# Layout of the reloaded product spectra: group of four token tiles ahead of sequence half

## The chip, the cores and the metric

The kernel runs on 1 core of one Trainium2 chip. The metric is the device time of one execution in microseconds (us); lower is better.

## The reference

One layer works on a sequence of 2048 tokens of 512 channels, in bfloat16:

```python
x = A_u                                   # (1, 2048, 512)
xn = _layernorm(x, axis=-1)
return x + A(xn) + B(xn)

# A: a state space convolution along the sequence, for each channel
P = exp(dt * A_cplx * l)                  # (512, 128, 2048): 128 modes
K = einsum("dn,dnl,dn->dl", C, P, dt * B).real
Yf = rfft(xn.T, padded to 4096) * rfft(K, padded to 4096)
y = irfft(Yf)[:, :2048].T + xn * Dskip

# B: a gated feed-forward of width 1792
h = sigmoid(xn @ w_gate) * (xn @ w_up)
y = h @ w_down
```

## The kernel before, in words

Three streams of work are woven into one program. The feed-forward runs over 4 groups of 512 tokens: gate matmuls (line 1030), up matmuls (line 1054), their products, and down matmuls (line 1098). The filter's spectrum is generated on the chip. The convolution is done with transforms written as matmuls. The step that matters here is its last one, the inverse transform.

**Products.** For each half of the channels (`p`, 0 or 1, 256 channels each) and each of 8 steps `u`, the product spectrum is made on TensorE (line 935), copied out of PSUM by ScalarE or VectorE (helper lines 283 and 285), and stored to a scratch tensor `v_scr` in HBM (dma helper, line 417). The inverse transform needs the same numbers with another index on the partitions, so they are read back in another order. This is the "reload".

**Reload.** The buffer `vall` lies at the start of `big`, the one large SBUF tile out of which most temporary buffers are cut by byte offset. It has, for each partition, `p`, a sequence half `j` (2), a token tile `i` (16) and 256 channels: 32 KB per partition. The reload comes in 12 transfers. There are three parts (`VPART`): part 0 is channel half 0 on all 128 partitions (512 KB a transfer), part 1 is channel half 1 on partitions 0 to 95 (384 KB), part 2 is channel half 1 on partitions 96 to 127 (128 KB). Each part has four transfers, one for each group of four token tiles; below "group 0" is tiles 0 to 3, "group 3" is tiles 12 to 15. A transfer brings both sequence halves of its four tiles: for each partition two pieces of 2 KB, one for each `j`.

**Inverse transform.** `s2_mm` (line 989) makes one token tile: for each `j` one matmul of 64 output rows (line 994), which reads tile `i` of both channel halves at once, 2 x 256 numbers that lie 16 KB apart. Tiles 12 to 15 get one matmul more (line 996). `final` makes two tiles: four matmuls into a pair of PSUM banks, then an addition on VectorE (line 1009), then the store of the result. Tiles 12 to 15 are added to the down matmuls' banks instead (lines 1104 and 1108), and VectorE adds the input (line 1118).

**Order.** `ORDER` lists all operations by hand in the order in which they are issued; each engine and each DMA queue takes its own in that order and never overtakes. For the reload, the SyncE queue (SP) has in this order: part 0 groups 2, 3, 0; part 2 groups 0, 2; part 1 groups 0, 3, 2; then part 0 group 1 and part 1 group 1; product stores stand between the first of them, and stores of the result behind the last. Part 2 groups 3 and 1 are on ScalarE's queue. TensorE's last operations are, in this order: 28 down matmuls; tiles 2 and 3 (group 0, four matmuls); tile 12 (group 3); tiles 0 and 1 (group 0); tile 13; tiles 8 and 9 (group 2); 14 down matmuls; tiles 6, 7, 4, 5 (group 1); tiles 14, 15; tiles 10 and 11; 28 half-width down matmuls.

**Waits.** Nobody writes a wait in this kernel. The tile framework compares the stretches of memory that two operations touch, and where they overlap and one of them writes, it makes the later one in the program wait for the earlier one. A wait of a DMA stands at the head of its queue and holds all transfers behind it.

Of the kernel before, what the change touches and what calls it, by code (L numbers as in the profile page):

```python
# [13 lines left out]
ACT = mybir.ActivationFunctionType  # L14
# [9 lines left out]
NT = 16  # L24
# [12 lines left out]
NP, DW = 2, 256  # L37
# [260 lines left out]
def _rate(pkt):  # L298

    pkt = min(pkt, 2048)  # L300
    return 16e3 * pkt / (pkt / 26.5 + 8.5)
# [14 lines left out]
def kernel(  # L316
# [12 lines left out]
    V, S, T, P, Y = nc.vector, nc.scalar, nc.tensor, nc.gpsimd, nc.sync  # L329
# [47 lines left out]
    def at(off, shape, dt=BF):  # L377
        assert off % 32 == 0
        n = int(np.prod(shape)) * (4 if dt == F32 else 2)
        assert off + n <= NBIG, (off, n)  # L380
        v = big[:, off // 2:(off + n) // 2]
        if dt == F32:
            v = v.bitcast(F32)
        if len(shape) > 1:
            ax = ["a%d" % i for i in range(len(shape))]
            v = v.rearrange("p (%s) -> p %s" % (" ".join(ax), " ".join(ax)), **dict(zip(ax[1:], shape[1:])))
        return v

    o = 0
# [7 lines left out]
    s2 = at(OFF["tmp"], [2, 64])  # L397
# [11 lines left out]
    def dma(q, dst, src, deps=(), prio=0.0, acq=(), rel=(), pkt=1024, after=None, hv=0.5):  # L409

        n = None
        get = lambda v: v() if callable(v) else v
        holder = {}

        def fn():
            with nc.allow_non_contiguous_dma(reason="laid out"):
                holder["i"] = QUEUE[q].dma_start(out=get(dst), in_=get(src))
            if after:
                after(holder["i"])

        return lambda nbytes: pl.add(q, 0.62, fn, deps, prio, acq, rel, dma=(nbytes, _rate(pkt), hv))
# [324 lines left out]
    for c in range(4):  # L746
# [10 lines left out]
        n = 1  # L757
# [214 lines left out]
    o_rt = pl.add("PE", 0.32, f_rt, [o_rz], 60, acq=[slr])  # L972
    o_rz = pl.add("ACT", 0.48, lambda slr=slr: S.activation(out=rr[0:8, :], in_=bank(slr)[0:8, :], func=ACT.Identity), [o_rt, l_sr, m_rr], 60, rel=[slr])

    vall = at(0, [NP, 2, NT, DW])
    vl = []
    for t in range(0, 8, 2):
        lds = []
        for n, (p, u0, u1) in enumerate(VPART):
            v_v = v_scr[n][:].rearrange("g q d -> (g q) d").rearrange("(p j i) d -> p j i d", j=2, i=NT)  # L980
            lds.append(dma("ACT" if n == 2 and t % 4 else "SP", vall[16 * u0:16 * u1, p, :, 2 * t:2 * t + 4, :], v_v[:, :, 2 * t:2 * t + 4, :],
                           deps=v_st[n] + table_free, prio=20 + n + 0.01 * t, pkt=2048, hv=0.9)(64 * KB * (u1 - u0)))
        vl.append(lds)
    vp_op = [vl[t // 2] for t in range(8)]
# [4 lines left out]
    def s2_mm(t, r, o, start, w):  # L989
        kw = dict(stop=True, skip_group_check=True)  # L990
        i = 2 * t + r
        ps = slice(w[0] // DW, w[1] // DW)
        for j in range(2):
            T.matmul(o[64 * j:64 * j + 64, :], s2[:, r, :], vall[:, ps, j, 2 * t + r, :], start=start, tile_position=(0, 64 * j), **kw)  # L994
        if i >= 12:
            T.matmul(o[64:128, :], sr[:, i - 12, :], rr[:, w[0]:w[1]], start=False, tile_position=(0, 64), **kw)

    def final(t, gdeps):
        sl, osl = _Slot("s"), _Slot("ot")
        ot = lambda: at(TAIL["ot"] + osl.idx * 2 * KB, [2, D])  # L1000

        def fy():
            for r in range(2):
                s2_mm(t, r, bank(sl, r), True, (0, D))
        my = pl.add("PE", 0.45, fy, vp_op[t] + [l_s2], 30 + t * 0.01, acq=[sl], mode="H")

        def fe():
            res = glu_sb[:, 2 * t:2 * t + 2, :] if t < 4 else at(TAIL["glu"] + 2 * KB * (t - 4), [2, D])
            V.tensor_tensor(out=ot().rearrange("p r d -> p (r d)"), in0=two(sl), in1=res.rearrange("p r d -> p (r d)"), op=ALU.add)  # L1009
        fin = pl.add("DVE", 1.13, fe, [my] + gdeps, 30, acq=[osl], rel=[sl])  # L1010
        isl = slice(2 * t, 2 * t + 2)
        dma("SP", outv[:, isl, :], lambda: ot(), deps=[fin], prio=1, rel=[osl], pkt=2048)(256 * KB)

    for grp in range(4):
# [63 lines left out]
        for jj in range(4):  # L1078
# [10 lines left out]
            r = jj % 2  # L1089
# [3 lines left out]
            def f2(i, po, c, start):  # L1093
                s2_mm(i // 2, i % 2, bank(po)[:, 0:c[1] - c[0]], start, c)
# [92 lines left out]
```

## Time and profile before

| what | value |
|---|---|
| median of 3 runs (lowest to highest) | 246.4 us (246.3 to 247.63) |
| profiled execution's own time | 246.36 us |
| its span, first to last instruction | 244.4 us |
| mean granted TensorE clock | 0.955 |
| TensorE matmul busy | 222.4 us, 91% |
| VectorE / ScalarE busy | 205.6 us, 84% / 174.7 us, 71% |
| GpSimd busy | 18.6 us, 8% |
| reload transfers `big<-v_scr` in the chain that ended last | 7% of the span |

Times in the profile count from the start of the span. "SPq" and "ACTq" are the sequencers of SyncE and ScalarE, where DMAs are issued; "PE" is TensorE, "DVE" VectorE, "ACT" ScalarE, "POOL" GpSimd. In the chain of waits a row is start, length, and what the time went to; a DMA's length there runs from its issue until its data have landed. A row of the timeline is start, length, engine, line, operation, tiles, count, and in brackets the idle time ahead of it and what ended it.

### The profile page before, as it was taken

How to read it: one execution, taken by the hardware profiler on the slowest of the kernel's cores; microseconds unless marked ns; L12 is line 12 of the kernel's file. 1: busy time of each engine (PE TensorE's matmuls, PEld its weight loads, DVE VectorE, ACT ScalarE, POOL GpSimd, SP SyncE). 2: the span in 40 equal slices, each digit the busy share in tenths (PEclk: the TensorE clock that was granted, in tenths of full speed). 3: DMA queues.
4: the chain of work that ended last, by engine and by line, in shares of the span. 5: the costliest groups of instructions: out<-in, count | busy, mean ns of one | idle time of the engine just before them, and what ended most of it. 6: DMA issues, size and time to landing. Idle time of an engine off the chain costs nothing.

```text
span 244.4 us, 5428 instructions
## 1 busy us (share of the span) xinstructions
PE 222.4 (91%) x2120; PEld 112.4 (46%) x2120; DVE 205.6 (84%) x448; ACT 174.7 (71%) x282; POOL 18.6 (8%) x42
## 2 busy tenths in 40 slices
PE   7969999999999999999999999999999999801694
PEld 3544444444444464465555664565536554300243
DVE  3999889999999999999999999997999998002264
ACT  5598999999999975859999778657888965000000
POOL 1240110300000020001000300000250000000000
PEclk9997999999999999999999999999999999965598
DMA  6995069961562163199356798366886766334234
GB/s 193 348 381 183 1 159 256 329 175 58 144 189 87 43 167 96 26 245 246 95 163 172 196 206 217 96 158 170 236 227 174 239 207 173 90 129 106 88 143 159
DMA packets 44091, 41.36 MB, mean 169 GB/s; under 512 B 8993, under 2 KB 36002, under 8 KB 44066
## 3 DMA queue, kind: packets, MB, share of 16 engines
q1 hardware_dynamic: 42898, 39.12, 54.2%
q0 software_dynamic: 864, 1.57, 4.0%
q10 hardware_dynamic: 304, 0.33, 0.5%
q8 instruction: 16, 0.26, 0.4%
q14 instruction: 9, 0.07, 0.1%
HBM read 25.28 MB, written 12.06 MB: 153 GB/s over the span
## 4 chain that ended last, share of the span: by engine, by line
PE 80%; DMA 10%; ACT 4%; DVE 2%; SPq 1%; issue 1%; POOL 0%; DVEq 0%; ACTq 0%; POOLq 0%
PE bank L1054 18%; PE bank L1098 18%; PE bank L1030 17%; DMA big<-v_scr 7%; PE pair L913 6%; PE pair L819 4%; PE bank L523 4%; PE pair L935 3%; PE pair L891 2%; PE pair L994 2%; DMA big<-big 2%; PE pair L1030 1%; PE pair L839 1%; ACT big L285 1%; DMA v_scr<-big 1%; PE pair L695 1%
## 5 line engine op out<-in xcount | busy, mean ns | idle before, releaser
L285 ACT ACTIVATE big<-pair 128x1024 bf16<-128x1024 f32 (+2 forms) x74 | 73.1, 994 | 16.6 <-PE pair L913 3.9
L1054 PE MATMUL bank<-xnT,wu_sb 128*128 128x512 bf16 x224 | 54.9, 380 | 0.0
L1030 PE MATMUL bank<-xnT,wg_sb 128*128 128x512 bf16 (+1 forms) x220 | 52.4, 377 | 2.4 <-ACT xnT L573 2.4
L1098 PE MATMUL bank<-wd_sb,hT_sb 128*128 128x512 bf16 (+1 forms) x238 | 50.7, 370 | 0.1
L1030 PEld LDWEIGHTS <-wg_sb 128*128 128x128 bf16 x236 | 22.9, 100 | 27.7 <-issue 6.0
L1098 PEld LDWEIGHTS <-hT_sb 128*128 128x128 bf16 x238 | 22.9, 98 | 26.4 <-issue 3.2
L1054 PEld LDWEIGHTS <-wu_sb 128*128 128x128 bf16 x224 | 20.3, 98 | 24.7 <-issue 3.7
L1042 ACT ACTIVATE hT_sb<-bank 128x512 bf16<-128x512 f32 x52 | 30.5, 618 | 1.2 <-PE bank L1030 1.1
L734 DVE TENSOR_TENSOR big<-big 128x1024 bf16<-128x1024 bf16 (+4 forms) x40 | 25.8, 645 | 1.0 <-ACT big L663 0.6
L735 DVE TENSOR_TENSOR big<-big 128x1024 bf16<-128x1024 bf16 (+4 forms) x40 | 25.8, 644 | 0.0
L1009 DVE TENSOR_TENSOR big<-pair,glu_sb 128x1024 bf16<-128x1024 f32 x4 | 4.8, 1223 | 23.9 <-PE pair L994 23.9
L918 DVE TENSOR_TENSOR big<-big 128x2048 bf16<-128x2048 bf16 x16 | 19.5, 1221 | 0.8 <-DMA big<-big 0.4
L913 PE MATMUL pair<-big 128*128 128x256 bf16 x160 | 19.7, 273 | 0.0
L1069 DVE TENSOR_TENSOR hT_sb<-hT_sb,bank 128x512 bf16<-128x512 bf16 x27 | 18.0, 679 | 0.6 <-ACT big L285 0.6
L913 PEld LDWEIGHTS <-big 128*128 128x128 bf16 x160 | 15.7, 98 | 4.8
L1065 ACT ACTIVATE us_sb<-bank 128x512 bf16<-128x512 f32 x29 | 17.7, 612 | 0.0
L739 DVE TENSOR_TENSOR big<-big 128x512 bf16<-128x512 bf16 (+4 forms) x40 | 16.9, 423 | 0.2
L740 DVE TENSOR_TENSOR big<-big 128x512 bf16<-128x512 bf16 (+4 forms) x40 | 16.8, 419 | 0.0
L787 ACT ACTIVATE sq_sb<-big 128x256 bf16<-128x256 bf16 (+2 forms) x20 | 12.8, 644 | 5.1 <-DVE big L740 4.9
L285 ACT ACTIVATE big<-big 128x256 bf16<-128x256 bf16 x31 | 12.5, 440 | 3.3 <-PE pair L819 3.3
L904 DVE COPY big<-big 32x1024 bf16<-32x1024 bf16 x32 | 14.0, 438 | 0.5
L935 PE MATMUL pair<-big 64*64 64x512 bf16 (+1 forms) x256 | 13.4, 327 | 0.5 <-DVE big L922 0.5
(107 smaller groups left out, 248.0 us busy)
## 6 DMA issues: line engine op xcount, KB each, us to landing
big<-c_E SPq DMA_DIRECT2D x16, 320.0 KB, 4.1
z_scr<-big SPq DMA_DIRECT2D x16, 256.0 KB, 2.9
big<-z_scr SPq DMA_DIRECT2D x16, 256.0 KB, 4.7
v_scr<-big SPq DMA_DIRECT2D x16, 256.0 KB, 3.0
big<-in_A_u_dram SPq DMA_DIRECT2D x4, 512.0 KB, 8.7
big<-big SPq DMA_DIRECT2D x32, 64.0 KB, 3.4
big<-v_scr SPq DMA_DIRECT2D x4, 512.0 KB, 4.8
wu_sb<-in_B_w_up_dram SPq DMA_DIRECT2D x2, 896.0 KB, 11.1
```

The source lines that it names most:

```text
L285: nc.scalar.activation(out=get(out), in_=get(in_), func=ACT.Identity)
L734: V.tensor_tensor(out=wide(outp), in0=wide(lo), in1=mre, op=ALU.mult)
L735: V.tensor_tensor(out=wide(tb()), in0=wide(lo), in1=mim, op=ALU.mult)
L913: T.matmul(two(sk)[:, o:o + DW], es()[:, g, kt, :], kT[p][:, kt, :], start=kt in (0, NKT - 1), stop=kt >= NKT - 2)
L918: V.tensor_tensor(out=pp().rearrange("p q h m -> p (q h) m"), in0=xx().rearrange("p q h m -> p (q h) m"), in1=kb()[:, 0:2 * DW].unsqueeze( ...
L935: T.matmul(two(sv)[o:o + 64, DW * (2 * g + y):2 * DW * (g + 1)], mab[b:b + 64, 2 * u + g, q, :], pq()[b:b + 64, q, ch] if y else pp()[b:b ...
L1030: T.matmul(bank(sl, k % 2)[:, c0:c1], w[:, kt, k * 128:(k + 1) * 128], xnT[:, grp, kt, c0:c1], start=(kt == 0), stop=(kt == KT - 1))
L1042: S.activation(out=hT_sb[:, hs.idx, k % 2, :], in_=bank(sl), func=ACT.Sigmoid)
L1054: T.matmul(bank(sl), wu_sb[:, kt, k * 128:(k + 1) * 128], xnT[:, grp, kt, :], start=(kt == 0), stop=(kt == KT - 1))
L1065: S.activation(out=us_sb[:, us.idx, :], in_=bank(sl), func=ACT.Identity)
L1069: V.tensor_tensor(out=h(), in0=h(), in1=us_sb[:, us.idx, :] if on else bank(sl), op=ALU.mult)
L1098: T.matmul(bank(po)[:, 0:c[1] - c[0]], hT_sb[:, hts[k // 2].idx, k % 2, jj * 128:(jj + 1) * 128], wd_sb[:, k, c[0]:c[1]], start=first and ...
```

## The change

The buffer `vall` gets another order of its indices: channel half, group of four token tiles, sequence half, tile within the group, channel. The two 2 KB pieces of a reload transfer, which lay 8 KB apart in a partition, now lie side by side as one piece of 4 KB. The matmul's read is moved to the new place; it still reads 2 x 256 numbers 16 KB apart. Source, sizes, number and order of the transfers, and all else stay.

```diff
-    vall = at(0, [NP, 2, NT, DW])
+    vall = at(0, [NP, 4, 2, 4, DW])
...
-            lds.append(dma("ACT" if n == 2 and t % 4 else "SP", vall[16 * u0:16 * u1, p, :, 2 * t:2 * t + 4, :], v_v[:, :, 2 * t:2 * t + 4, :],
+            lds.append(dma("ACT" if n == 2 and t % 4 else "SP", vall[16 * u0:16 * u1, p, t // 2], v_v[:, :, 2 * t:2 * t + 4, :],
...
-            T.matmul(o[64 * j:64 * j + 64, :], s2[:, r, :], vall[:, ps, j, 2 * t + r, :], start=start, tile_position=(0, 64 * j), **kw)
+            T.matmul(o[64 * j:64 * j + 64, :], s2[:, r, :], vall[:, ps, t // 2, j, 2 * (t % 2) + r, :], start=start, tile_position=(0, 64 * j), **kw)
```

## The prediction

> **What bounds the kernel now.** I read the windows first, to see in which stretch TensorE, the busiest engine, is not busy. Columns: stretch, its length, busy time (instructions) of PE, PEld, DVE, ACT, POOL, granted clock, DMA share, GB/s.
>
> ```profile
> 186.00:206.50 20.50, 20.30 (x200) 10.51 (x197) 20.13 (x39) 15.81 (x21) 0.00 (x0) 1.00 0.73 214
> 212.80:220.50 7.70, 0.38 (x1) 0.00 (x0) 0.00 (x0) 0.00 (x0) 0.00 (x0) 0.69 0.31 102
> 221.60:228.00 6.40, 0.00 (x0) 0.00 (x0) 1.23 (x1) 0.00 (x0) 0.00 (x0) 0.50 0.73 184
> 228.00:231.60 3.60, 3.58 (x15) 1.27 (x16) 1.23 (x1) 0.00 (x0) 0.00 (x0) 0.50 0.00 0
> 231.60:235.30 3.70, 3.70 (x17) 1.40 (x16) 2.42 (x3) 0.00 (x0) 0.00 (x0) 0.84 0.47 177
> ```
>
> Until 206.5 TensorE is full (20.30 of 20.50). Then come two holes of 7.7 and 6.4 us in which no engine does anything to speak of, and behind them a stretch at half clock. The chain of waits says what fills the holes:
>
> ```profile
> 205.24 3.00 DMA v_scr<-big
> 208.24 0.02 issue
> 208.25 4.54 DMA big<-v_scr
> 212.79 0.02 issue
> 212.81 3.76 DMA big<-v_scr
> 216.57 0.02 issue
> 216.59 3.73 DMA big<-v_scr
> 220.32 0.25 issue
> 220.56 1.05 PE pair L994 x3
> 221.61 0.02 issue
> 221.63 0.56 SPq L417
> 222.19 0.04 issue
> 222.23 5.75 DMA big<-v_scr
> 227.98 0.04 issue
> 228.02 0.64 PE bank L994
> ```
>
> The last product store lands at 208.24. Then part 1 is reloaded group by group (0, 3, 2), each transfer issued 0.02 us after the one ahead of it has landed. Tiles 2 and 3 end at 221.61, and only then the reloads of group 1 go out; they land at 227.98. The waits of SP's queue and of TensorE in this stretch, and TensorE's timeline:
>
> ```profile
> SPq L417 <- DMA big<-v_scr: 7.2, 2, 4.0
> SPq L417 <- PE pair L994: 4.4, 1, 4.4
> ...
> PE pair L994 <- DMA big<-v_scr: 7.4, 1, 7.4
> PE bank L994 <- DMA big<-v_scr: 6.4, 1, 6.4
> ...
> 210.82 1.89 PE L1098 MATMUL bank<-wd_sb,hT_sb 128*128 128x512 bf16 x8
> 212.83 0.38 PE L994 MATMUL pair<-big 128*64 128x512 bf16 x1
> 220.56 1.03 PE L994 MATMUL pair<-big 128*64 128x512 bf16 x3 [7.35 <-DMA big<-v_scr]
> ```
>
> The first of the four matmuls of tiles 2 and 3 (sequence half 0) ran at 212.83, right behind group 0's landing. The second (sequence half 1) needs the same transfer and no other, yet waited until group 2 had landed at 220.32. So the waits are not those of the data. They fit one rule: the tile framework takes an access of two pieces as all bytes from its lowest to its highest. Group g of a part covers [2g, 2g+2] KB and [8+2g, 10+2g] KB; taken from end to end, all four groups overlap, each reload waits for the one before, and a read at sequence half 1 seems to touch groups 2 and 3. For the same reason part 0 group 1 waits for the reads of tiles 2 and 3, and holds part 1 group 1 behind it in the queue.
>
> **The change, part by part.** (1) *Reloads among themselves.* Each now writes one piece of 4 KB, [4g, 4g+4] KB of its channel half; no two overlap, so the waits between them go. Part 1's groups 3 and 2 are issued right behind group 0, which still waits for the last store (208.25). An issue costs SP this much:
>
> ```profile
> 208.25 0.57 SPq L417 DMA_DIRECT2D big<-v_scr  x1
> ```
>
> so they go out at about 208.8 and 209.4 in place of 212.81 and 216.59. (2) *Reads of tiles 2 and 3.* In part 1 they lie, by the same end-to-end rule, in groups up to their own, so they wait for group 0 alone: TensorE goes on at 212.81 with all four. At full clock eight matmuls of this length took 1.89 us and the last alone 0.38, so 0.216 each; four take 3 x 0.216 + 0.38 = 1.03 us and end at 213.84.
>
> (3) *What is late next: group 1.* The matmul reads both channel halves, which still lie 16 KB apart. End to end, tiles 2 and 3 cover from group 0 of channel half 0 to group 0 of channel half 1, and part 0's group 1 lies in between. So I keep this false wait: part 0 group 1 is issued when tiles 2 and 3 are done, 213.86 in place of 221.63. And tile 12 (group 3), next on TensorE, seems to touch groups 0 to 3 of channel half 1, so it still waits for part 1's group 1, the last to land. From the first of these two issues to the last landing it was 227.98 - 221.63 = 6.35 us. I take the same: 220.21, and tile 12 starts at 220.25 in place of 228.02, 7.77 us earlier. Both the store of tiles 2 and 3 and the clock are then where they were relative to it: TensorE was idle 6.4 us ahead of 228.02 and restarted at 0.50, and would again be idle from 213.84 to 220.25.
>
> (4) *Everything behind tile 12*, 228.02 to the end of the span, keeps its order and its waits, so it moves as a block.
>
> ```profile
> core 0: 244.4 us, clock 0.955
> ```
>
> (5) *Reloads before 208.* SP waited there too, for instance 2.0 us ahead of part 0 group 3, and ScalarE's queue for its two of part 2:
>
> ```profile
> SPq L417 <- DMA big<-v_scr: 2.0, 1, 2.0
> ...
> 205.52 3.92 ACTq L417 DMA_DIRECT2D big<-v_scr  x2
> 209.54 0.59 ACT L973 ACTIVATE big<-pair 8x512 bf16<-8x512 f32 x1 [3.80 <-DMA big<-v_scr]
> ```
>
> These waits go and the transfers move forward by 2 to 3 us. I cost that at nothing: TensorE's own work up to 206.5 covers it, and the last product store hangs on TensorE and ScalarE, not on SP's freedom. Without the cover it would be worth at most those 2.0 us; against that, 128 KB more of part 2 run beside the last store. (6) *The 4 KB piece.* The source still has two 2 KB pieces for each partition. No row shows such a transfer. The nearest, at 512 KB: pieces of 4 KB from a constant, and the reload in its old form twice.
>
> ```profile
> big<-c_MAB SPq DMA_DIRECT2D x1, 512.0 KB, 5.7
> ...
> big<-v_scr SPq DMA_DIRECT2D x1, 512.0 KB, 4.4
> ...
> big<-v_scr SPq DMA_DIRECT2D x1, 512.0 KB, 5.5
> ```
>
> So between -1.1 and +1.3 us for one transfer; two stand one after the other on the path, hence -2.2 to +2.6. I take 0, since old form and 4 KB pieces lie within the spread of the old form alone. (7) *TensorE's reads* at other addresses, same stride: nothing.
>
> *The sum:* 246.36 - 7.77 = 238.6 us, against the profiled execution's own time, which is 0.04 below the median of the runs. If group 0 lands as fast as its two successors did (3.73 and 3.76 us, with no part 2 beside it), TensorE itself is the limit (free at 210.82 + 1.89 = 212.71): 0.1 less.
>
> **Does it pay to have them in flight together?** Alone, 384 KB took 3.75 us; the last pair, 896 KB in flight together, took 6.35 us. So 512 KB more cost 2.6 us, 0.0051 us per KB, against more than 4 us as a transfer of its own. Overlap pays in this kernel. By that price all five transfers (2048 KB) end no earlier than 208.25 + 3.75 + 1664 x 0.0051 = 220.5, which is 0.3 behind the 220.21 above: the DMA engines are nearly the limit, and the sum could be 238.9. [...]
>
> **Rivals.** *Interleaving delays group 0 (chance 0.08).* Groups 3 and 2 share the engines with group 0, which TensorE needs first. At worst all three land together: 3.75 + 768 x 0.0051 = 7.65 us after 208.25, at 215.9. Then tiles 2 and 3 end at 216.95, group 1 lands at 223.3, tile 12 starts 4.7 us earlier than before: 241.7 us. Against it: they are in one queue, issued 0.57 us apart. The pair, though, landed with the earlier one close to the later.
>
> *Reads are compared piece by piece (0.13).* If a single-piece write against a two-piece read is seen as it is, group 1 waits for nobody, all five are issued by 210.6, and tile 12 needs only group 3. Then tiles 12, 0, 1, 13, 8, 9 and the 14 down matmuls run while group 1 comes in, and TensorE stands at the pair that began at 235.35 when group 1 lands at 220.5:
>
> ```profile
> 231.64 3.71 PE bank L1098 x14
> 235.35 0.98 PE pair L994 x8
> ```
>
> 14.9 us earlier, 231.5 us. For it: only two-piece against two-piece is seen to be taken end to end. Against it: the read of tiles 2 and 3 has its pieces 16 KB apart, and the compiled program of before makes its first matmul wait also for part 0's group 3, which no piece of that read touches.
>
> *The waits stay (0.05).* If they came from the queue and not from the layout, nothing moves: 246.4. Against it: part 2's first transfer was not held for part 0's in the same queue, which landed only at 196.53 + 4.2:
>
> ```profile
> 196.53 0.53 SPq L417 DMA_DIRECT2D big<-v_scr  x1
> ...
> 198.72 0.62 SPq L417 DMA_DIRECT2D big<-v_scr  x1
> ...
> big<-v_scr SPq DMA_DIRECT2D x1, 512.0 KB, 4.2
> ```
>
> *The other side: the reload gets slower (0.02).* If the unequal shapes of source and destination made each transfer slower by a factor f, the path is 208.25 + 4.54 f + 1.07 + 6.35 f + 0.04; it meets 228.02 at f = 1.71. At f = 2 it is 3.1 us later than before: 249.5. Against it: the 4 KB constant took 5.7 us, a factor 1.3 at most.
>
> **How the numbers follow.** The forecast of one remaining false wait holds 0.72, and the four rivals 0.08, 0.13, 0.05 and 0.02. The time is 238.6. Its own bounds: -2.2 to +2.6 by item 6, and the clock: if TensorE came back at full speed, the stretches at 0.50 and 0.84 would lose 1.8 and 0.6, 2.4 us. So 236.2 to 241.2, and to 241.7 with the first rival; that holds 0.80 and leaves out the piece-by-piece case below and the two above. A change under 0.5% (1.2 us) can't be told from none in this kernel. Faster: 0.72 + 0.08 + 0.13 = 0.93; same: 0.05; slower: 0.02.
>
> **What would show it.** In the chain of waits: one `big<-v_scr` from 208.25 in place of three; part 1's three issues 0.6 us apart; all four matmuls of tiles 2 and 3 together near 213; part 0's group 1 issued right behind their end, near 213.9; one hole of about 6.4 us on TensorE that ends near 220.2 with the landing of part 1's group 1; the stretch behind it at half clock; a span near 236.6. Wrong would be: tile 12 starting before group 1 has landed, part 0's group 1 issued before tiles 2 and 3 are done, or the three landings at one time near 216.

## The result and the profile after

The changed kernel took 238.06 us (median of 4 runs, 237.38 to 239.56) against 247.01 us of the kernel before in runs beside it; the ratio is 0.9655, with a 95% interval of 0.9586 to 0.9724. The ratio leaves out slow runs, here one of 251.24 us of the kernel before, and so do all ratios below. In a later call with more rounds it was 239.2 us, ratio 0.9701 (0.9674 to 0.9729). The profiled execution took 237.75 us, 8.61 less than that of before.

The chain of waits of the changed kernel, from the tail on (start, length, what it went to):

```profile
206.27 6.15 PE bank L1098 x28
212.42 0.09 issue
212.51 0.64 PE pair L994 x4
213.14 0.02 issue
213.16 0.56 SPq L417
213.72 0.04 issue
213.76 6.39 DMA big<-v_scr
220.16 0.14 issue
220.29 0.64 PE bank L994 x2
```

Of the three reloads that stood here one after the other, none is left. TensorE itself leads to 212.42, because the down matmuls end just as group 0 lands. Tiles 2 and 3 run in one go, and their end releases group 1's pair; then comes one wait for part 1's group 1, up to tile 12. The timeline of TensorE has the one hole that is left:

```profile
212.51 0.62 PE L994 MATMUL pair<-big 128*64 128x512 bf16 x4
220.29 0.64 PE L994 MATMUL bank<-big 128*64 128x512 bf16 x2 [7.16 <-DMA big<-v_scr]
```

Windows of the changed kernel (stretch, length, busy time of PE, PEld (TensorE's weight loads), DVE, ACT, POOL with counts, granted clock, DMA share, GB/s):

```profile
206.50:212.80 6.30, 6.21 (x32) 2.65 (x30) 0.00 (x0) 0.59 (x1) 0.00 (x0) 1.00 0.67 175
212.80:220.00 7.20, 0.33 (x4) 0.00 (x0) 1.23 (x1) 0.00 (x0) 0.00 (x0) 0.74 0.87 224
220.00:224.00 4.00, 3.55 (x16) 1.68 (x18) 1.62 (x2) 0.00 (x0) 0.00 (x0) 0.62 0.01 2
224.00:228.00 4.00, 4.00 (x28) 1.98 (x28) 2.73 (x4) 0.00 (x0) 0.00 (x0) 1.00 0.54 199
```

In its first hole the kernel before had the DMA engines at a share of 0.31 and 102 GB/s. Now the hole, of nearly the same length, has 0.87 and 224 GB/s, about twice the bytes: transfers that stood one behind the other in two holes run side by side in one. The issues of DMAs in windows that hold one or two of them (count, size, median from issue to landing):

```profile
big<-v_scr SPq DMA_DIRECT2D x1, 384.0 KB, 4.3
...
big<-v_scr SPq DMA_DIRECT2D x2, 384.0 KB, 5.6
...
big<-v_scr SPq DMA_DIRECT2D x1, 512.0 KB, 6.3
```

The first is group 0 alone, issued at 208.14; the second holds group 0 and group 3 (its median is the mean of the two, so group 3 took 6.8); the third is part 0's group 1.

From the first issue of part 1 to the start of tile 12 it was 19.77 us before (228.02 - 208.25) and is 12.15 now (220.29 - 208.14): 7.62 less. From tile 12 to the end of the span it was 16.38 and is 15.41: 0.97 less. The first issue is 0.11 earlier. Together that is the 8.7 us by which the span fell, 244.4 to 235.7 (span and mean granted clock of the core):

```profile
core 0: 235.7 us, clock 0.978
```

### The profile page after: what moved, and what is told of

It reads as the page before. It is cut to its first block, busy times and chain, and to the rows that moved or that the text cites. A ratio compares the mean times of both kernels' runs of the same rounds, so it can differ in the third digit from the quotient of the medians.

```text
span 235.7 us, 5403 instructions
## 1 busy us (share of the span) xinstructions
PE 218.3 (93%) x2092; PEld 112.2 (48%) x2120; DVE 205.6 (87%) x448; ACT 174.7 (74%) x282; POOL 18.1 (8%) x42
## 4 chain that ended last, share of the span: by engine, by line
PE 83%; DVE 5%; DMA 5%; ACT 4%; issue 2%; POOL 0%; SPq 0%; DVEq 0%; ACTq 0%; POOLq 0%
PE bank L1098 21%; PE bank L1054 18%; PE bank L1030 18%; PE pair L913 6%; PE pair L819 4%; PE bank L523 4%; PE pair L935 3%; DMA big<-v_scr 3%; DMA v_scr<-big 2%; PE pair L994 2%; PE pair L891 2%; PE pair L1030 1%; PE pair L839 1%; DVE hT_sb L1069 1%; DVE big L918 1%
## 5 line engine op out<-in xcount | busy, mean ns | idle before, releaser
L1054 PE MATMUL bank<-xnT,wu_sb 128*128 128x512 bf16 x211 | 53.7, 380 | 1.0 <-issue 0.5
L1030 PE MATMUL bank<-xnT,wg_sb 128*128 128x512 bf16 (+1 forms) x212 | 51.8, 377 | 2.9 <-ACT xnT L573 2.4
L1098 PE MATMUL bank<-wd_sb,hT_sb 128*128 128x512 bf16 (+1 forms) x233 | 49.5, 366 | 0.5 <-issue 0.3
L787 ACT ACTIVATE sq_sb<-big 128x256 bf16<-128x256 bf16 (+2 forms) x20 | 12.8, 645 | 4.4 <-DVE big L740 4.2
```

What stands on the lines that cost most here:

```text
L1030: T.matmul(bank(sl, k % 2)[:, c0:c1], w[:, kt, k * 128:(k + 1) * 128], xnT[:, grp, kt, c0:c1], start=(kt == 0), stop=(kt == KT - 1))
L1054: T.matmul(bank(sl), wu_sb[:, kt, k * 128:(k + 1) * 128], xnT[:, grp, kt, :], start=(kt == 0), stop=(kt == KT - 1))
L1098: T.matmul(bank(po)[:, 0:c[1] - c[0]], hT_sb[:, hts[k // 2].idx, k % 2, jj * 128:(jj + 1) * 128], wd_sb[:, k, c[0]:c[1]], start=first and ...
```

## The experiments

Two questions were open. Does the gain come from the waits between reloads, as predicted, or from the one contiguous piece? And is the wait that remains, tile 12's, a false one as the prediction says, or just the time that the DMA engines need? The start of the tail moves by up to 2.6 us between two executions of the same kernel (207.48 and 210.07 with the group index outermost), so each profile is also read from part 1's first issue. All times are medians. The diffs show the lines that carry the change; "..." stands for what is left out.

**Two pieces that do not overlap.** A gap of 32 B is put between the two pieces of a reload (`vall` indexed as channel half, group, sequence half, 1040 values of which 1024 are used); the buffers behind `vall` move by 512 B, and transfer and read are moved to the new places.

```diff
-    vall = at(0, [NP, 4, 2, 4, DW])
+    vall = at(0, [NP, 4, 2, 1040])
...
```

> The changed kernel with 32 bytes left free between the two pieces of each transfer (and the buffers behind moved by 512 bytes): two pieces of 2 KB again, but no two transfers overlap end to end. Overlap theory (the gain is the waits that went because the transfers' stretches no longer overlap): as the changed kernel, 238.1 us, ratio to before about 0.966, part 1's three issues 0.6 us apart. Contiguity rival (the gain is that each transfer writes one piece of 4 KB): most of the gain is lost, 244 to 247 us.

Measured: 237.46 us, ratio 0.9647 (0.9609 to 0.9686), the time of the changed kernel. Contiguity brings nothing. The page of the changed kernel says the same from another side: its line on packets is that of before in number and size classes, because the source still comes in 2 KB pieces.

```profile
DMA packets 44091, 41.36 MB, mean 175 GB/s; under 512 B 8993, under 2 KB 36002, under 8 KB 44066
```

**The layout of before, with each reload as two transfers.** Each transfer writes one 2 KB piece, so writes don't overlap from end to end, and the reads are those of before.

```diff
-    dma(..., vall[16 * u0:16 * u1, p, :, 2 * t:2 * t + 4, :], v_v[:, :, 2 * t:2 * t + 4, :], ...)
+    for j in range(2):
+        dma_start(out=vall[16 * u0:16 * u1, p, j, 2 * t:2 * t + 4, :], in_=v_v[:, j, 2 * t:2 * t + 4, :])
```

> The layout of before, but each reload is issued as two transfers, one for each sequence half, so that each of them writes one 2 KB piece of a partition; the reads are those of before. Theory (what is compared is the stretch from the first to the last byte of an access, of writes and of reads alike): the reloads no longer wait for each other, and part 1's six issues follow each other about 0.6 us apart from 208; but tile 2's second matmul, which reads the second half of both channel halves, spans the first half of part 1 in groups 3 and 2, so it waits for five of the six transfers, to about 216.5; tiles 2 and 3 end near 217.3, group 1's four transfers follow and land about 7 us later, tile 12 starts near 224.4, 4.1 us later than in the changed kernel: about 242. Rival 1 (only the mutual waits of the reloads cost, the reads do not): tiles 2 and 3 near 213, and the time of the changed kernel, about 238, plus at most 1.5 for the additional issues. Rival 2 (five more issues of 0.6 us on SP, and more descriptors in flight, eat the overlap): 245 or more, with issues that lie further apart than 0.7 us.

Measured: 238.3 us, ratio 0.9646 (0.9585 to 0.9707), where 242 was expected. The mechanism is there, line by line. Its timeline of TensorE:

```profile
212.21 0.40 PE L997 MATMUL pair<-big 128*64 128x512 bf16 x1
214.55 0.59 PE L997 MATMUL pair<-big 128*64 128x512 bf16 x3 [1.94 <-DMA big<-v_scr]
```

Its chain of waits (the variant issues its reloads from a line of its own, 984):

```profile
209.71 4.71 DMA big<-v_scr
214.42 0.14 issue
214.55 0.61 PE pair L997 x3
215.16 0.17 SPq L984
...
215.86 4.33 DMA big<-v_scr
220.19 0.04 issue
220.24 1.07 PE bank L997 x2
```

Tile 2's second matmul waited for the fifth of part 1's six transfers, and group 1 was issued only behind it, 2 us later than in the changed kernel. That did not delay tile 12, which started at 220.24. Six half transfers landed by 214.95, and group 1's four, issued behind them, followed by 220.68. My price for them was wrong (I had put the fifth landing at 216.5 and group 1 at 224.4). The end of the span came 1.5 us later from the first issue than in the changed kernel (29.07 against 27.56): TensorE ran at half clock until 225.98 in place of 223.07, of which more below. Together with the run before, this shows that the waits among reloads were the cost, whichever way they are taken away.

**Reads of tiles 2 and 3 split by channel half**, so that part 0's group 1 no longer waits for them; all other reads as in the changed kernel.

```diff
-    T.matmul(o[64 * j:64 * j + 64, :], s2[:, r, :], vall[:, ps, ...], ...)
+    for q in ([ps] if t != 1 else [slice(q, q + 1) for q in range(ps.start, ps.stop)]):
...
+        T.matmul(o[64 * j:64 * j + 64, c], s2[:, r, :], vall[:, q, ...], ...)
```

> The changed kernel, with the read split for tiles 2 and 3 alone. Part 0 group 1 then waits for nobody and goes out near 210.0 behind groups 3 and 2; tile 12 still waits for part 1 group 1. If the late issue of group 1 is what costs: group 1 lands 3 us earlier, 235 us. If the DMA engines are the limit by then (five transfers, 2048 KB, by 0.0051 us per KB beyond the first): group 1 lands near 219.9 in place of 220.2, 237.7 us, no measurable change against the changed kernel's 238.1.

Measured: 239.36 us, ratio 0.9702 (0.9646 to 0.9759): no gain. The issues do go out one behind the other, and the last needs 9.08 us in place of 6.39:

```profile
212.85 0.04 issue
212.89 0.60 SPq L417
213.49 0.04 issue
213.54 9.08 DMA big<-v_scr
222.62 0.14 issue
222.75 0.64 PE bank L996 x2
```

All five reloads landed 11.63 us after the first issue (210.99), against 12.02 in the changed kernel (208.14 to 220.16). It was run again beside the changed kernel:

> The changed kernel once more, side by side with the three variants below, because the start of the tail moves by up to 3 us from one execution to another. All theories: 238 us, a ratio of 0.965 to the kernel before.

> The reads of tiles 2 and 3 split by channel half once more. Theory (2048 KB of reloads need 12 us from the first issue of part 1, however they are queued): within 0.6 us of the changed kernel of the same call. Rival (issuing group 1 earlier helps, and the first profile was only a late start): 1 to 2 us faster.

Measured: the changed kernel 239.2 us, ratio 0.9701 (0.9674 to 0.9729), the split one 237.8 us, ratio 0.9649 (0.962 to 0.9677). This time it was 1.4 us ahead; over all calls the runs that enter the ratios have medians of 238.8 (ten of the changed kernel) and 237.95 (nine of the split one). Counted from the first issue, tile 12 starts 0.4 to 0.5 us earlier in the split kernel's two profiles than in the changed kernel's two (table below). Whether this wait is worth nothing or up to 1.4 us of the time stays open; it isn't worth the 3 us by which the issue of group 1 moved, counted from the first issue (212.89 - 210.99 = 1.90 us behind it, against 213.16 - 208.14 = 5.02).

**All other reads split, those of tiles 2 and 3 not.** Now tile 12 needs only group 3, and part 0's group 1 waits as in the changed kernel.

```diff
+    for q in ([ps] if t == 1 else [slice(q, q + 1) for q in range(ps.start, ps.stop)]):
...
```

> The changed kernel, with the read of both channel halves split into two matmuls of 256 columns for all tiles but 2 and 3. Tile 12 then needs group 3 alone, while part 0 group 1 still waits for the reads of tiles 2 and 3 (issue near 213.2). Overlap theory, if the false wait of tile 12 is what costs: group 1 still lands near 220.2, but tiles 12, 0, 1, 13, 8, 9 and the 14 down matmuls run meanwhile; tiles 6, 7 start near 221.1: about 232.5 us, nearly all that the kernel with the group outermost gets. If the late issue of group 1 is what costs: within 1 us of the changed kernel's 238.1.

Measured: 232.6 us, ratio 0.9423 (0.9375 to 0.947), as expected. Tile 12's first matmul, which reads channel half 0, ran at 213.10, and the next waited only for part 1's group 3, landed at 214.14. Group 1, which landed at 219.96, was hidden behind the other tiles and the 14 down matmuls but for 0.53 us. The timeline of TensorE in this kernel:

```profile
214.19 0.30 PE L996 MATMUL bank<-big 128*64 128x256 bf16 x2 [0.81 <-DMA big<-v_scr]
...
220.01 0.95 PE L996 MATMUL pair<-big 128*64 128x256 bf16 x14 [0.53 <-DMA big<-v_scr]
```

And its chain of waits behind that:

```profile
215.34 1.24 DVE big L1011
216.57 0.02 issue
216.59 4.44 DMA out_dram<-big
...
221.66 1.23 DVE big L1011
```

The tail now hangs on VectorE's additions and on the stores of the result that free their buffers.

**The group index outermost**, ahead of the channel half: then a read of one group, from its first to its last byte, touches no other group.

```diff
-    vall = at(0, [NP, 4, 2, 4, DW])
+    vall = at(0, [4, NP, 2, 4, DW])
+    home = lambda t: (t // 2 + 2) % 4
...
```

> Group of four tiles made the outermost index (order in memory 2, 3, 0, 1), channel half second: a read of both channel halves now stays end to end within its own group, so nothing waits for a group that it does not touch. Overlap theory: group 1's transfers go out at about 210.0 and 210.6 in place of 213.16 and 213.76; tile 12 starts with group 3's landing (about 215.6), tiles 8 and 9 with group 2's (217.4), the 14 down matmuls run meanwhile, and tiles 6, 7 start near 221.1 in place of 226.6: about 232.5 us. Bandwidth rival (what is left of the hole is the DMA engines' time and not waits): within 1 us of the changed kernel's 238.1.

> The group index outermost once more. All theories: 4 to 5 us faster than the changed kernel of the same call, since tile 12 no longer waits for group 1.

Measured: 233.15 us, ratio 0.9445 (0.94 to 0.949), and 232.39 us, ratio 0.9412 (0.937 to 0.9453). The false wait of tile 12 is worth 5 to 7 us. Part of that is the clock: the changed kernel's two profiles run at half clock for 2.8 and 4.0 us behind the start of tile 12, which costs half of that, while four of the five profiles of the kernels in which tile 12 needs only its own group show full clock there. In its timeline tile 12 waits 1.48 us for its own group 3, and group 1 is no longer waited for:

```profile
214.74 0.62 PE L995 MATMUL pair<-big 128*64 128x512 bf16 x4 [0.94 <-issue]
216.84 0.41 PE L995 MATMUL bank<-big 128*64 128x512 bf16 x2 [1.48 <-DMA big<-v_scr]
```

**Part 0 of group 1 moved forward in the written order**, right behind part 0 of group 0, once in the changed kernel and once with the group index outermost (twice). Only the number 582 moves in `ORDER`.

```diff
-    ... 489, 506, 579, 490, ...   ... 675, 676, 582, 583, 922, ...
+    ... 489, 506, 579, 582, 490, ...   ... 675, 676, 583, 922, ...
```

> The changed kernel, with one reload moved in the written order: part 0 of group 1 stands right behind part 0 of group 0 (issue near 193.5), so that it no longer has to wait until tiles 2 and 3 have read, and part 1 of group 1 is issued right behind the other three of part 1. Theory (the landing of group 1 sets tile 12, and the DMA engines set that landing): 1536 KB are left behind 208.1 instead of 2048, by the 0.0059 us per KB of the kernel with the group index outermost (five transfers from 210.07 to 222.06) 9 us, so the landing is near 217.1, tile 12 starts 3.1 us earlier than in the changed kernel, and the time is about 235.0. Rival 1 (the 512 KB moved ahead hold up the stores behind which part 1 waits): the last store lands later than 208.1 by up to 2.6 us, and the time is 237 to 238. Rival 2 (the order of TensorE's work behind tile 12 and the other engines set the end): no gain, 238.

> The kernel with the group index outermost, with part 0 of group 1 moved right behind part 0 of group 0 as in the run beside it. Theory: no read waits for a group that it does not use, and all of part 1 is on its way from 208.1; tile 12 waits only for its own group 3, whose landing was 2.1 us behind group 0's, and that wait of 1.48 us shrinks to nothing or stays, since group 3 still shares the engines; tiles 6 and 7 find group 1 long landed. 231 to 233, against 233.15 without the move. Rival (the tail is by now bound by the down matmuls and by VectorE behind them): no change at all, 233.

> The group index outermost and part 0 of group 1 early, once more. Theory (tile 12 waits for the landing of its own group 3, which shares the engines with 1536 KB in place of 2048 KB): 0.5 to 1.8 us faster than the kernel beside it that has only the group index outermost. Rival (the tail is bound by VectorE and the down matmuls): within 0.4 us of it.

Measured in the changed kernel: 235.97 us, ratio 0.9553 (0.9485 to 0.9621), where 235.0 was expected. Part 1's four reloads were issued together and the last landed 8.90 us after the first issue (208.77), with tile 12 right behind it:

```profile
210.73 6.95 DMA big<-v_scr
217.67 0.14 issue
217.81 0.41 PE bank L994 x2
```

So 512 KB less in flight bring that landing forward by 12.02 - 8.90 = 3.1 us, 0.0061 us per KB. Against the split kernel, in which no reload of group 1 is held back either, it is 11.63 - 8.90 = 2.7 us. With the group index outermost the move brought nothing that can be told: 231.29 us, ratio 0.9346 (0.9277 to 0.9415), in one call, but 232.97 us, ratio 0.9419 (0.9367 to 0.9471), beside 232.39 without the move in the other. There the rival was right: group 1 isn't waited for any more, so it does not matter when it lands.

A table by part 1's first issue, from the profile of each kernel (us):

| kernel | first issue | last reload landed | tile 12 starts | end of span |
|---|---|---|---|---|
| before | 208.25 | +19.73 | +19.77 | +36.15 |
| changed (first, second profile) | 208.14, 208.83 | +12.02, +12.14 | +12.15, +12.28 | +27.56, +28.27 |
| 32 B gap | 207.77 | +11.51 | +11.65 | +27.63 |
| two transfers each, old layout | 207.93 | +12.75 | +12.31 | +29.07 |
| tiles 2, 3 split (first, second profile) | 210.99, 208.66 | +11.63, +11.66 | +11.76, +11.79 | +27.21, +27.34 |
| group 1 early | 208.77 | +8.90 | +9.04 | +24.73 |
| all but tiles 2, 3 split | 207.38 | +12.58 | +6.81 | +22.72 |
| group outermost (first, second) | 210.07, 207.48 | +11.99, +10.74 | +6.77, +6.65 | +22.53, +21.12 |
| group outermost, group 1 early (first, second) | 208.38, 208.72 | +8.94, +9.13 | +6.75, +6.61 | +21.02, +21.18 |

Wherever five reloads (2048 KB) are not made to wait for each other, the last lands 10.7 to 12.8 us after the first issue, whenever group 1 is issued. What differs is whether tile 12 has to wait for it, and behind tile 12 the clock: the two profiles with the group index outermost end 1.4 us apart, and the first of them ran at half clock from 217.16 to 220.58, the second not at all there.

## Why the prediction was right, point by point

The forecast was 238.6 us, the profiled execution took 237.75 and the median was 238.06. Its mechanism was the right one; the sizes of three terms were off.

- *Reloads among themselves (1).* Right. The three issues are at 208.14, 208.75 and 209.39, predicted 208.25, 208.8 and 209.4. The gap and the two-transfer experiment show that this alone carries the gain.
- *Reads of tiles 2 and 3 (2).* Right in kind: all four run behind group 0's landing, and end at 213.14 in place of 213.84. The four took 0.64 us, not 1.03: I had priced them by down matmuls, one after the other, and three of them had taken 1.05 at half clock before. At full clock four take 0.62 on the timeline, less than four times 0.216, so the two halves' 64-row matmuls share the time.
- *Group 1 (3).* Its waits are as predicted: part 0's group 1 was issued behind tiles 2 and 3, and tile 12 waited for part 1's group 1. The pair took 7.00 us from its first issue (213.16 to 220.16) in place of 6.35, while groups 3 and 2 were still on their way (to 215.58 and 217.40). That shortfall cancels the 0.70 us by which tiles 2 and 3 were early. That the two cancel fits the experiments: both the split of tiles 2 and 3 and the two-transfer kernel say that the landing is set by the DMA engines' work since 208, hardly by the moment of issue. The step that the prediction made its path, the release by tiles 2 and 3, is true in the program and little of the price; the side remark that five transfers end no earlier than 220.5 names the actual limit, a little too late (measured 220.16; 12.25 us from the first issue by that remark, 10.7 to 12.8 over the kernels). It was luck that the summed path, 220.21, lay within 0.3 us of that limit.
- *What an earlier issue is worth.* The Trainium skill's page "DMA: Bandwidth & Descriptors", section "Issuing engines are not separate DMA queues", says that DMAs run on the same 16 engines and interleave, whichever engine started them, and that starting them from several engines at once saves only the time of initiating them. It has no rule for several transfers in flight from one queue, which is the case here: three reloads took 12.07 us in turn (208.25 to 220.32) and 7.0 to 9.3 us together. Where the engines already have a share of 0.87, little is left to gain: group 1, issued 3 us earlier relative to the first reload, landed 0.4 to 0.5 us earlier.
- *Everything behind tile 12 (4).* It did not move as a rigid block: 15.41 us in place of 16.38. TensorE came back at 0.50 in both kernels. Windows of one us of the kernel before, and then of the changed one, show when it was back at full clock:

```profile
231.00:232.00 1.00, 1.00 (x4) 0.15 (x3) 0.57 (x2) 0.00 (x0) 0.00 (x0) 0.50 0.00 0
232.00:233.00 1.00, 1.00 (x4) 0.38 (x3) 1.00 (x2) 0.00 (x0) 0.00 (x0) 0.60 0.70 262
```

```profile
221.50:222.50 1.00, 1.00 (x8) 0.49 (x5) 0.20 (x1) 0.00 (x0) 0.00 (x0) 0.50 0.00 0
222.50:223.50 1.00, 1.00 (x6) 0.29 (x3) 1.00 (x1) 0.00 (x0) 0.00 (x0) 0.71 0.00 0
223.50:224.50 1.00, 0.84 (x5) 0.50 (x6) 0.93 (x2) 0.00 (x0) 0.00 (x0) 1.00 0.07 25
```

  The rows beside them have 0.50 and 1.00, so a mean of 0.60 means full clock for the last 0.2 us, from 232.8, 4.8 us behind the restart at 228.02; a mean of 0.71 means it from 223.1, 2.8 us behind 220.29. Those 2.0 us less at half clock save 1.0 us. This is the mis-sized term that made the time 0.9 us lower than the sum; the range had a place for it. The traces also show why the clock came back sooner. The whole stretch at half clock, most of it in the holes, in the kernel before and in the changed one:

```profile
215.72:232.80 17.08, 5.81 (x20) 1.86 (x21) 3.57 (x3) 0.00 (x0) 0.00 (x0) 0.50 0.39 111
```

```profile
216.24:223.08 6.84, 2.79 (x13) 1.41 (x14) 0.78 (x1) 0.00 (x0) 0.00 (x0) 0.50 0.45 130
```

  These are five and two times 3.41 us. In the two-transfer kernel the stretch runs from 215.74 to 225.98 (10.24 us, three times), in the changed kernel with group 1 early from 218.13 to 221.55 (3.41 us, once). So in these traces the clock changes in steps of 3.41 us, and the delay depends on where in a step the work restarts. In the changed kernel 2.78 us of the step that ended at 223.07 were busy, and that was enough. In the kernel before, 1.36 us of the step that ended at 229.38 were not, nor 2.32 us of the one that ended at 222.56 in the two-transfer kernel; both had to run one more step at half clock. Where in a step tile 12 would start could not be foreseen from the profile of before, so this gain of 0.9 us is luck. The Trainium skill's page "TensorE: Matmul & The Clock Gate", section "What's actually happening", says that activity is judged in windows of about 3.4 us that run freely and don't start with the work, so that the moment of the change depends on where a window is met. The traces agree.
- *Reloads before 208 (5).* SP's reloads ahead of part 1 did go out 0.3 to 3.2 us earlier (part 0's group 0 at 193.36 in place of 196.53), and part 1's first issue moved by 0.11 us only. That fits a worth of nothing, but the first issue wanders by more than that between executions (208.14 and 208.83 in the changed kernel).
- *The 4 KB piece (6).* Zero was right, but for a simpler reason than I gave: no such piece exists on the way, since the packets did not change.
- *Rivals.* Interleaving did not delay group 0 against before: 4.28 us from issue to landing with two reloads behind it, where it was 4.54, both with a transfer of part 2 beside it. The waits didn't stay, and no reload got slower by itself. Reads are not compared piece by piece; the kernels with the reads split or the group index outermost, in which tile 12 waits only for its own group, took 232.4 to 233.2 us, near the 231.5 of that rival.

## What to carry to other kernels

When several DMAs fill one buffer, look at the stretch from the first to the last byte that each access covers: pieces that interleave make the framework order transfers that have nothing to do with each other, and the sign in the profile is a queue that waits for its own previous transfer while the DMA share is near 0.3. Do the same for the reads, since a matmul that reads two far pieces also waits for all that lies between; here that was worth another 5 to 7 us, and putting the index by which work is released outermost removed both. Before moving an issue forward, add up the bytes: with a DMA share near 0.9 an earlier issue of the same bytes bought 0.4 to 0.5 us of landing here, and 512 KB less in the critical stretch 2.7 to 3.1 us.

## What was not expected of the hardware

Transfers in flight together landed one after the other in the order of issue. In the kernels with whole reloads the first of three of the same size took 4.3 to 5.2 us, with the end of a transfer of part 2 beside it, and the third 6.0 to 8.0; alone, such a reload took 3.73 to 3.76. A reload alone kept the DMA engines at about a third (0.33 and 103 GB/s in the window of group 3 before), so on average two thirds of the engines' time in its 3.75 us went unused:

```profile
212.80:216.60 3.80, 0.38 (x1) 0.00 (x0) 0.00 (x0) 0.00 (x0) 0.00 (x0) 0.89 0.33 103
```

The same three reloads (1152 KB) needed 9.3 us in the changed kernel (8.4 in its second profile), 7.2 with the 32 B gap and 7.0 as six half transfers, though in the first two the issues are spaced alike; group 1's pair then landed 11.5 to 12.8 us from the first issue in all three. What the engines did differently there stays open.
